# Gating the second pair of start-up loads and reordering the software loads in a fused window-attention and feed-forward kernel

## The chip, the cores and the metric

The kernel runs on one core of one Trainium2 chip. The metric is the device time of one launch in microseconds (us). Before the change it is 303.25 us, the median of four runs (303.24, 303.24, 303.26 and 303.73).

## The reference, cut to what matters

Batch 8, 8 heads, 576 positions, head size 64. Attention sees a window of 32 positions on either side. Its output, 4608 tokens of width 512, goes through a feed-forward pair with a squared ReLU between the two products.

```python
scores = q @ k.T / sqrt(64)                      # per batch and head
scores = where(abs(i - j) <= 32, scores, -1e9)
x = softmax(scores) @ v                          # -> (4608, 512), heads side by side
h = x @ w_in                                     # 512 -> 2048
out = (maximum(h, 0) ** 2) @ w_out               # 2048 -> 512, float32
```

## The kernel before, in words

Attention is cut into 72 chunks of 64 tokens (nine per batch element), the feed-forward part into nine tiles of 512 tokens (T = 0 to 8). An 8th of a tile's x is one chunk.

For a piece of tokens, K and Q (float32 in memory) are loaded with tokens on partitions, turned by TensorE (`tok_turn`, L489) and copied to `kt` by VectorE (L505) and to `qt` by ScalarE (L502) in the first batch element. Scores of a chunk or of two chunks are 8 or 16 small matmuls (L585), ScalarE takes the exponential (L605), VectorE multiplies with the mask (L614), TensorE multiplies with V (L720 and L721), VectorE divides by the row sum (L731, L733) and TensorE and ScalarE turn the result into `xt` (L749, L755). For odd chunks V is needed shifted by 64 partitions: VectorE copies it from `vx` to `vd` (L543, `vd_half`). The first feed-forward tile is made of 16 blocks of 16 matmuls (`mm1_small`, L768): block (g, q) takes 128 tokens (two chunks) and a quarter q of `w_in`; ScalarE's ReLU (L776) and VectorE's square (L824) follow. Then comes the second product (L861), which needs the quarters of `w_out`.

All work is recorded first (`Prog.rec`, L62) with the engine, a planned duration, tags of what it reads and writes, and a key. A planner (`schedule`, L265, with `forward`, L98) simulates five engines and the DMA queues with the durations and the `move` numbers of the loads, tries several priorities, and keeps the order per engine that its own model likes best. After that the order on each engine is fixed: every engine runs its list in order and waits on semaphores. Planned gaps on TensorE up to the first product's dense stretch are filled with idle matmuls on zeros (`fill`, L306, issued as L410); their number follows from the plan, not from what happens on the chip.

Loads use three queues. SyncE (SP) and ScalarE (ACT) issue hardware-queue loads: `first_load` (L449, issued at L454) brings K and Q of piece 0 (96 tokens) and of piece 2 (128 tokens) in float32 into staging tiles (`oe` for piece 0, `pf` for piece 2). GpSimd (POOL) issues all the other loads of batch elements 0 and 1, which convert to bfloat16 on the way: K and Q pieces (L461), V pieces (L531) and the quarters of the two weights (L548, L553). Their order on POOL is the list ORDER (L34): `k03` is K of batch 0, piece 3 in numbers from 0, `w10` the first quarter of `w_in`, `w20` that of `w_out`, and so on. Keys below -100 are kept as they are, so POOL issues them in that order. In batch 0 the pieces are 96, 64, 128, 128, 128 and 32 tokens of K and Q (L38), and 96, 128, 128, 128 and 96 of V (L39). `build` (L895) records all of it.

Before the change both hardware loads of a queue are issued one straight after the other at the start.

Of the kernel before, what the change touches and what calls it, by code (L numbers as in the profile page):

```python
# [30 lines left out]
PADS, MARGINS, ROUNDS, NREP = (0, 1000, 2000), (0, 4000, 8000), 3, 4  # L31
LATE = {"POOL": 1500, "SP": 2000, "ACT": 2000}
DEPTH, POST, BACK = 4000, {"POOL": 1500, "SP": 1000, "ACT": 1000}, {"POOL": 2500, "SP": 4000, "ACT": 4000}
ORDER = ("k01 q01 v00 v01 v02 w10 k03 q03 v03 k04 q04 v04 w11 w12 w13 k05 q05 k10 q10 v10 k11 q11 v11 "  # L34
         "w20 w21 w22 w23 k12 q12 v12 k13 q13 v13 k14 q14 v14").split()
GT0, WT0 = (12.5, 16, 20, 25.5), (13, 18, 23, 26)
TURN0 = {1: 1, 2: 2, 4: 3, 6: 4}
# [321 lines left out]
class Gen:  # L359
# [86 lines left out]
    def slot(self, b, x):  # L446
        return 512 * (x if b else x - 1)

    def first_load(self, t, x, eng, key):  # L449
        t0, n = PIECE0[x]  # L450
        src = (self.q if t == "q" else self.k)[0, :, t0:t0 + n, :].rearrange("h p d -> p h d")
        stg, o, w, tag = self.STG[t, x]
        dst = bass.AP(stg, o, [[w, n], [64, 8], [1, 64]])
        self.p.rec(eng, lambda e: e.dma_start(dst, src), writes=[tag], dma=(f"s{t}{x}", 0), key=key, dur=420, move=(n // 2, 14, 1500 if x == 0 else 2500))  # L454

    def tok_load(self, b, t, x, key):
        t0, n = self.pieces(b)[x]
# [88 lines left out]
    def load_w1(self, d, key):  # L546
        src = self.w_in[:, 512 * d:512 * d + 512].rearrange("(f p) c -> p f c", p=128)
        self.p.rec("POOL", lambda e: e.dma_start(self.W1[:, :, 512 * d:512 * d + 512], src),  # L548
                   writes=[("w1", d)], dma=(f"w1{d}", 0), key=key, dur=770, move=(32, 82 if d else 130, 500))

    def load_w2(self, d, key):
        src = self.w_out[512 * d:512 * d + 512, :].rearrange("(k p) c -> p k c", p=128)
# [342 lines left out]
    def build(self):  # L895
        p = self.p
        self.k1 = self.grp = 0
        self.group, self.bank = {}, {}

        K = -200.0  # L900
        self.setup_idle()
        self.setup_masks(K - 20)
        self.setup_rest(0, K + 3)
        self.setup_ptz(0, K + 2)
        self.setup_ptz(1, K + 2)
        self.setup_ptz(2, K + 2)
        self.setup_rest(1, -20)
        at = {it: K + 1 + k for k, it in enumerate(ORDER)}
        for d in range(4):
            self.load_w1(d, at[f"w1{d}"])  # L910
            self.load_w2(d, at[f"w2{d}"])

        tile = 0
        for b in range(B_):
            while 8 * tile + 7 < NCH * b:
                self.moe(tile)
                tile += 1
            if b < FB:
                if not b:
                    for x in (0, 2):  # L920
                        self.first_load("k", x, "SP", -300 + x)
                        self.first_load("q", x, "ACT", -300 + x)
                for bb in range(0 if b else FB):
                    for x in range(6):
                        for t in "kqv":
                            if f"{t}{bb}{x}" not in at:
                                continue
                            if t == "v":
                                self.vx_load(bb, x, at[f"v{bb}{x}"])
                            else:  # L930
                                self.tok_load(bb, t, x, at[f"{t}{bb}{x}"])
            else:
                for x in range(5):
                    kb = 9 * b - 40 + 2 * x
                    for t in "kq":
                        self.tok_load(b, t, x, kb)
                        self.dma_turn(b, t, x, 9 * b - LEAD - 9 + 2 * x)
                    self.vx_load(b, x, kb + 0.1)
            for c in range(NCH):
                n = NCH * b + c  # L940
                if b >= TB:
                    if c % 3 == 0:
                        if b == 1 and not c:
                            for x in range(2):
                                self.tok_turn(1, x, n - LEAD - 3)
                        self.scores(n, 3)
                        if c == 3:
                            self.vd_half(b, 1, 3, n - LEAD, [("sc", n)])
                        self.av3(n, 0)
                        self.av3(n, 1)  # L950
                        y = (n // 3) % 2
                        self.evac3(n, y)
                        if b == 1 and c < 6:
                            for x in range(2, 4) if not c else (4,):
                                if x < TX:
                                    self.tok_turn(1, x, n - LEAD)
                                else:
                                    for t in "kq":
                                        self.dma_turn(1, t, x, n - LEAD)
                        self.xturn3(n, y)  # L960
                    continue
                m = 1 if not c or n in (1, 8) else 2
                if n not in self.group:
                    if n == 0:
                        self.tok_turn(0, 0, -LEAD - 3)
                    if n == 8:
                        self.moe(0)
                        tile = 1
                        self.tok_turn(0, 5, -LEAD + 5)
                    self.scores(n, m)  # L970
                    if n + m < TB * NCH and n + m != 8:
                        bb, cc = divmod(n + m, NCH)
                        self.tok_turn(bb, (cc + 1) // 2 if bb else TURN0[cc], n + m - LEAD - 3)
                if c % 2 and not b:
                    x = (c + 1) // 2
                    self.vd_half(b, x - 1, x, n - LEAD - 3)
                if b and not self.group[n][1]:
                    odd = [c + u for u in range(self.group[n][2]) if (c + u) % 2]
                    if odd:
                        self.vd_half(b, odd[0] // 2, odd[-1] // 2 + 1, n - LEAD, [("sc", n)])  # L980
                self.av(n)
                gi, k, m = self.group[n]
                if n < 2:
                    self.evac(n, 1, 0, n)
                    if n:
                        self.xturn(0, 2, 0)
                elif k == m - 1:
                    self.evac(n - k, m, gi, 0)
                    self.xturn(n - k, m, gi)

        for T in range(tile, NT + 1):
            self.moe(T)
        p.schedule()
        with self.nc.Block():
            dsems, dcount = p.emit()
            for s in dsems:
                if s[0] == "o":
                    self.nc.sync.wait_ge(dsems[s], dcount[s])
# [32 lines left out]
```

The softmax here doesn't subtract the row's maximum and nothing guards it: scores larger than these inputs give would overflow.

## Time and profile before

| what | value |
|---|---|
| median of the runs shown | 303.25 us |
| the profiled execution's own time | 302.34 us |
| its span, first to last instruction | 300.5 us |
| outside the span | 1.84 us |
| TensorE busy | 293.9 us (98%) |
| VectorE, ScalarE, GpSimd busy | 176.3, 159.9, 105.0 us |
| idle matmuls (L410) | 114, 10.3 us, all between 1.0 and 17.4 us |
| TensorE busy from 25 us to 200 us | 175.0 of 175.0 us |
| software DMA queue | 113120 packets, 17.9 MB |

The profile is one execution with the time of every instruction. "Idle before" is time in which an engine waited ahead of an instruction, with what released it. TensorE counts as busy when it runs idle matmuls too, so in the first 25 us a busy engine is not a useful one. An issue of a load stands on the engine that issues it; a load has landed when its semaphore is complete, which is what the consumer waits for.

Landings in the profiled execution, in us from the start of the span: K and Q of piece 0 at 4.5 and 5.0; of piece 2 at 6.8 and 7.6; k01 7.9, q01 8.1, v00 8.7, v01 9.6, v02 10.4, w10 12.8, k03 13.6, q03 15.4, v03 15.9, k04 16.8, q04 17.6, v04 18.3, w11 20.8, w12 23.3, w13 25.9, w20 33.9, w21 36.6, w22 39.2, w23 42.0, k12 42.7, q12 43.5.

### The profile page before, as it was taken

Reading aid. Unit: us, or ns where it says so; the run is one execution under the profiler, and the core shown is the slowest. Engines: PE = TensorE matmul, PEld = TensorE weight load, DVE = VectorE, ACT = ScalarE, POOL = GpSimd, SP = SyncE. Lnnn points to the kernel's source line nnn. Section 1 sums busy time; section 2 is a strip of 40 time slices with the busy share of each in tenths; the row PEclk is TensorE's granted clock in tenths of the full one; section 3 lists DMA queues with packets and bytes.
Section 4 is the critical chain, followed back from the end, with each engine's and each line's share of the span. In section 5 each row is a group of like instructions: output and inputs, shape, how many; then the busy total and the mean of one; then the engine's idle time right before and its main releaser. Section 6 shows DMA issues by size and latency. Waiting matters only on the chain.

```text
span 300.5 us, 7083 instructions
## 1 busy us (share of the span) xinstructions
PE 293.9 (98%) x2796; PEld 172.1 (57%) x2796; DVE 176.3 (59%) x429; ACT 159.9 (53%) x267; POOL 105.0 (35%) x131
## 2 busy tenths in 40 slices
PE   7889999999999999999999999999999999999996
PEld 7679955866768754444444454444444444444445
DVE  5775656664998957757665596768457663222200
ACT  3457634656758645654565665557365554444411
POOL 8999842241515532452144644315410000000000
PEclk9999999999999999999999999999999999999999
DMA  9999999999999999999899999999992210100022
GB/s 147 174 194 170 206 174 194 170 142 192 175 139 135 122 186 159 129 132 164 141 115 133 156 163 163 130 170 107 158 156 81 79 26 35 37 35 36 35 84 93
DMA packets 166818, 39.34 MB, mean 131 GB/s; under 512 B 157825, under 2 KB 162305, under 8 KB 166785
## 3 DMA queue, kind: packets, MB, share of 16 engines
q0 software_dynamic: 113120, 17.90, 90.3%
q1 hardware_dynamic: 46512, 11.15, 25.6%
q10 hardware_dynamic: 7152, 9.83, 11.2%
q8 instruction: 22, 0.36, 0.5%
q14 instruction: 12, 0.09, 0.1%
HBM read 36.70 MB, written 9.44 MB: 154 GB/s over the span
## 4 chain that ended last, share of the span: by engine, by line
PE 94%; DMA 2%; DVE 2%; issue 0%; ACT 0%; POOL 0%; POOLq 0%; DVEq 0%
PE outp L861 41%; PE ht L809 28%; PE ht L791 7%; PE ht L768 7%; PE sc L585 3%; PE sc L645 3%; DMA kraw<-in_k_dram 2%; PE sc L489 1%; DVE vd L543 1%; PE outp L410 1%; PE sc L837 1%; PE outp L837 1%; DVE kt L505 0%; PE sc L693 0%; PE outp L749 0%
## 5 line engine op out<-in xcount | busy, mean ns | idle before, releaser
L861 PE MATMUL outp<-w,gt 128*128 128x512 bf16 x560 | 136.0, 379 | 0.0
L809 PE MATMUL ht<-xt,w 128*128 128x512 bf16 x384 | 94.5, 379 | 0.0
L824 DVE TENSOR_TENSOR gt<-rt 128x512 bf16<-128x512 bf16 x144 | 59.2, 418 | 58.9 <-ACT rt L815 51.0
L815 ACT ACTIVATE rt<-ht 128x512 bf16<-128x512 f32 x96 | 57.3, 599 | 57.0 <-PE ht L809 54.1
L861 PEld LDWEIGHTS outp<-w,gt 128*128 128x128 bf16 x560 | 52.7, 98 | 58.2
L809 PEld LDWEIGHTS ht<-xt,w 128*128 128x128 bf16 x384 | 36.5, 98 | 42.4
L461 POOL DMA_DIRECT2D qraw<-in_q_dram x39 | 33.2, 852 | 51.7 <-PE ht L809 24.2
L461 POOL DMA_DIRECT2D kraw<-in_k_dram x39 | 33.4, 857 | 44.1 <-PE ht L809 19.3
L605 ACT ACTIVATE e<-sc 128x512 bf16<-128x512 f32 (+1 forms) x48 | 37.4, 809 | 11.5 <-PE sc L585 11.5
L531 POOL DMA_DIRECT2D vx<-in_v_dram x40 | 34.4, 861 | 19.6 <-PE ht L809 10.9
L868 ACT ACTIVATE oe<-outp 128x512 f32<-128x512 f32 x35 | 20.9, 598 | 26.4 <-PE outp L861 26.3
L669 DVE TENSOR_TENSOR xr<-pf,rs 128x512 bf16<-128x512 f32 (+1 forms) x42 | 27.7, 682 | 0.4
L626 DVE TENSOR_TENSOR pt<-e,mask 128x512 bf16<-128x512 bf16 x42 | 17.6, 422 | 14.0 <-ACT e L605 13.9
L768 PE MATMUL ht<-xt,w 128*128 128x128 bf16 x384 | 24.1, 219 | 0.3 <-ACT xt L755 0.3
L791 PE MATMUL ht<-xt,w 128*128 128x256 bf16 x192 | 23.4, 273 | 0.0
L768 PEld LDWEIGHTS ht<-xt,w 128*128 128x128 bf16 x384 | 21.7, 98 | 0.8 <-ACT xt L755 0.5
L662 DVE COPY pf<-sc 128x520 f32<-128x520 f32 x21 | 14.7, 700 | 11.5 <-PE sc L645 11.2
L791 PEld LDWEIGHTS ht<-xt,w 128*128 128x128 bf16 x192 | 18.0, 98 | 3.3
L776 ACT ACTIVATE rt<-ht 128x512 bf16<-128x512 f32 x24 | 14.2, 599 | 10.3 <-PE ht L768 10.0
L659 ACT ACTIVATE pf<-sc 128x520 f32<-128x520 f32 x21 | 12.6, 601 | 11.8 <-PE sc L645 11.8
L797 ACT ACTIVATE rt<-ht 128x512 bf16<-128x512 f32 x24 | 14.4, 599 | 7.4 <-PE ht L791 7.1
L664 DVE TENSOR_TENSOR pf<-pf 64x520 f32<-64x520 f32 x21 | 14.6, 698 | 5.6 <-ACT pf L659 4.7
(78 smaller groups left out, 192.0 us busy)
## 6 DMA issues: line engine op xcount, KB each, us to landing
out_dram<-oe ACTq DMA_DIRECT2D x35, 256.0 KB, 3.6
kraw<-in_k_dram POOLq DMA_DIRECT2D x30, 128.0 KB, 5.7
qraw<-in_q_dram POOLq DMA_DIRECT2D x30, 128.0 KB, 5.4
vx<-in_v_dram POOLq DMA_DIRECT2D x24, 128.0 KB, 5.7
w<-in_moe_w_in_dram POOLq DMA_DIRECT2D x4, 512.0 KB, 10.4
w<-in_moe_w_out_dram POOLq DMA_DIRECT2D x4, 512.0 KB, 16.8
vx<-in_v_dram POOLq DMA_DIRECT2D x16, 96.0 KB, 5.8
xt<-xr SPq DMA_TRANSPOSE x36, 4.4
```

The source lines that it names most:

```text
L461: self.p.rec("POOL", lambda e: e.dma_start(dst, src), writes=[("fraw", b, t, x)], old=[("fraw", b - 2, t, y + (b == 2))], reads=self.pace( ...
L531: self.p.rec("POOL", lambda e: e.dma_start(self.VX[b % 2][r:r + n, s, :, 0:64], self.v[b, :, t0:t0 + n, :].rearrange("h p d -> p h d")), w ...
L605: self.p.rec("ACT", lambda e, d=dst, a=src: e.activation(d, a, ACTF.Exp, scale=0.125), reads=["s" + x for x in name], writes=[("e", h)], k ...
L626: self.p.rec("DVE", lambda e, a=pt, c=ee, d=mb: e.tensor_tensor(a, c, d, ALU.mult), reads=[("e", k // 2), "mask"], writes=[("ptt", k)], ol ...
L669: self.p.rec("DVE", lambda e, w=w, np=np: e.tensor_tensor(bass.AP(self.XR, 512 * (2 * y + w), [[2048, np], [64, 2], [128, 4], [1, 64]]), b ...
L768: mm = e.matmul(ht[:, 128 * (d % 4):128 * (d % 4) + 128], self.W1[:, ft, 128 * d:128 * d + 128], self.XT[:, ft, t0:t0 + 128], start=(ft == ...
L791: mm = e.matmul(ht[:, 256 * (d % 2):256 * (d % 2) + 256], self.W1[:, ft, 128 * d:128 * d + 128], self.XT[:, ft, 64 * s0:64 * s0 + 256], st ...
L809: mm = e.matmul(ht[:], self.W1[:, ft, 128 * d:128 * d + 128], self.XT[:, ft, 512 * T:512 * T + 512], start=(ft == 0), stop=(ft == 3))
L815: self.p.rec("ACT", lambda e: e.activation(rt[:], ht[:], ACTF.Relu), reads=[("ht", k % 2)], writes=[("rt", k % 4)], key=key, dur=560)
L824: self.p.rec("DVE", lambda e: e.tensor_tensor(g, r, r, ALU.mult), reads=[("rt", k % 4)], writes=tags, key=key, dur=430)
L861: mm = e.matmul(op, gt[:, d, 128 * u:128 * u + 128], self.W2[:, d, :], start=(d == 0), stop=(d == 15))
L868: self.p.rec("ACT", lambda e: e.activation(oe[:], op, ACTF.Copy), reads=[tag], writes=[("oe", x % 4)], key=key, dur=560)
```

## The change

The hardware load of piece 2 now waits, on each of the two queues, for the landing of the load of piece 0 on the same queue (the new argument `gate` makes it read the tag of the first staging tile). In ORDER, `k03 q03 v03` move ahead of `w10`, and `w11` moves ahead of `v04`. The planner is told a smaller cost for the first quarter of `w_in` (105 for 130). As the planner runs again with this, the order on all engines comes out new, mostly in the first 40 us.

```diff
-ORDER = ("k01 q01 v00 v01 v02 w10 k03 q03 v03 k04 q04 v04 w11 w12 w13 k05 q05 k10 q10 v10 k11 q11 v11 "
+ORDER = ("k01 q01 v00 v01 v02 k03 q03 v03 w10 k04 q04 w11 v04 w12 w13 k05 q05 k10 q10 v10 k11 q11 v11 "
...
-    def first_load(self, t, x, eng, key):
+    def first_load(self, t, x, eng, key, gate=()):
...
-        self.p.rec(eng, lambda e: e.dma_start(dst, src), writes=[tag], dma=(f"s{t}{x}", 0), key=key, dur=420, move=(n // 2, 14, 1500 if x == 0 else 2500))
+        self.p.rec(eng, lambda e: e.dma_start(dst, src), reads=gate, writes=[tag], dma=(f"s{t}{x}", 0), key=key, dur=420, move=(n // 2, 14, 1500 if x == 0 else 2500))
...
-                   writes=[("w1", d)], dma=(f"w1{d}", 0), key=key, dur=770, move=(32, 82 if d else 130, 500))
+                   writes=[("w1", d)], dma=(f"w1{d}", 0), key=key, dur=770, move=(32, 82 if d else 105, 500))
...
-                    for x in (0, 2):
-                        self.first_load("k", x, "SP", -300 + x)
-                        self.first_load("q", x, "ACT", -300 + x)
+                    self.first_load("k", 0, "SP", -300)
+                    self.first_load("q", 0, "ACT", -300)
...
+                if not b:
+                    self.first_load("k", 2, "SP", -298, [self.STG["k", 0][3]])
+                    self.first_load("q", 2, "ACT", -298, [self.STG["q", 0][3]])
```

In the order that the planner now gives (from the built program): on ScalarE the list begins with the load of piece 0, the gated load of piece 2, the load of the activation table, then the copy to `qt` of piece 0. On VectorE the copies L543 that wait for v00 and v01 stand ahead of the first masking L614. On TensorE the turning of piece 1 stands ahead of the first scores, the first two chunks are done ahead of Q of piece 2, and 86 idle matmuls are left of 114.

## The prediction

> **What bounds the kernel now.** I read the slices first, then TensorE's timeline of the first 25 us, then ScalarE's, then the DMA view by stretches.
>
> ```profile
> PE   7889999999999999999999999999999999999996
> ```
>
> From the fifth slice on TensorE is full, and the table by stretches has it busy 175 of 175 us from 25 to 200. The work after that is fixed, so the change can only move the moment at which the dense stretch begins. That beginning, on TensorE:
>
> ```profile
> 6.60 0.23 PE L410 MATMUL outp<-zz 128*128 128x128 bf16 x1
> 7.93 0.29 PE L489 MATMUL sc<-identw,kraw 64*128 64x64 bf16 x4 [1.09 <-DMA kraw<-in_k_dram]
> ...
> 8.60 1.04 PE L489 MATMUL ht<-oe,pf 128*128 128x128 f32 x8
> ...
> 10.93 0.41 PE L585 MATMUL sc<-qt,kt 64*128 64x64 bf16 x16
> ...
> 15.42 1.06 PE L768 MATMUL ht<-xt,w 128*128 128x128 bf16 x16
> 16.32 1.17 PE L410 MATMUL outp<-zz 128*128 128x128 bf16 x18
> 17.32 0.39 PE L489 MATMUL outp<-identw,kraw 128*128 128x128 bf16 x4
> ...
> 22.21 1.07 PE L768 MATMUL ht<-xt,w 128*128 128x128 bf16 x16
> ```
>
> The columns are start, length, what. TensorE waits for k01 until 7.9; the first feed-forward block stands at 15.42; then come idle matmuls until piece 3, whose q03 landed at 15.4; the second block is at 19.54 and the third, the first to need w11 (landed 20.8), at 22.21. From there TensorE doesn't stop. I measure everything by this third block.
>
> Two views show why k01 is late. By queue (packets, MB, share of the engines), between 4.5 and 5.5 us and between 8 and 9 us:
>
> ```profile
> q10 hardware_dynamic: 423, 0.11, 68.0%
> q1 hardware_dynamic: 412, 0.10, 67.0%
> q0 software_dynamic: 29, 0.00, 5.6%
> ```
>
> ```profile
> q0 software_dynamic: 1226, 0.15, 242.7%
> ```
>
> While the four hardware loads run, the software queue moves 29 packets in a microsecond; alone it moves 1226. A packet is one head of one token: k01 and q01 are 512 each, v00 768, v01, v02, k03 and so on 1024 (0.83 us at that rate). k01's last packet went at 6.7, although GpSimd had issued it by 2.2. ScalarE:
>
> ```profile
> 1.20 0.65 ACTq L454 DMA_DIRECT2D pf<-in_q_dram  x1
> 1.88 1.28 ACT L502 ACT_TABLE_LOAD   x1 [1.88 <-issue]
> 5.74 0.49 ACT L502 ACTIVATE qt<-ht 128x384 bf16<-128x384 f32 x1 [2.59 <-PE ht L489]
> ```
>
> The table load follows the second load's issue in ScalarE's list; today it is over at 3.2 and hidden.
>
> [...] Between 54.5 and 55 us it does (210 packets of q1, 209 of q0); between 4.5 and 5.5 it did not (835 to 29), and the output store issued at 45.55 behind a long software queue sent its first packet only at 49.5. So what entered first seems to go first, and the measurement decides. [...] The trace shows idle matmuls 112 ns apart in the first 4 us and 55 ns apart at 10 us, and no return after the 1.1 us wait.
>
> **The change part by part.**
>
> *Gate on SP.* Nothing else stands on SP's queue until its first transpose at 49 us, so the wait costs no one. K of piece 0 lands at 4.5; today 1.06 us pass from issue (0.74) to the first packet (1.80), so K of piece 2 starts near 5.6 and not 3.6.
>
> *Gate on ACT.* Queued behind it are the table load and everything after. Wait to 5.0, issue 0.65, table load 1.28: 6.95. The copy to `qt` of piece 0 moves from 5.74 to 6.95 and ends at 7.45; first scores 7.6 (today 6.38); exponential of chunk 0 8.0 to 8.55, of chunk 1, after scores at 8.65, 9.0 to 9.6. So the first masking can't be before 8.6.
>
> *Software queue.* The first loads' 1536 packets are through by 4.0. k01 (issued 1.35) then runs 4.0 to 4.45, q01 to 4.9, v00 to 5.5. Landing is 0.7 to 1.2 us after the last packet (v01: 8.64, 9.64), so k01 5.5, q01 5.9, v00 6.5. For v01 the trace has no case of a hardware load arriving at this point. It is issued at 3.6, and after idle stretches a software load starts 1.6 to 2.05 us later, so its first packet is at 5.2 to 5.65, just when K of piece 2 arrives. Bound below: v01 goes whole, last packet 6.4, landed 7.2 to 7.4. Bound above: it shares with both hardware loads to the end, last packet near 8.4, landed 9.4. I take the middle, V = 8.3 (today 9.6). All packets up to v02 are the same work as before, so v02 ends near 9.7 as today. After it: k03, q03, v03 without w10's 2.2 us ahead of them land at 11.4, 12.6, 13.2 (13.6, 15.4, 15.9); w10 behind those three lands at 15.4 (12.8); k04, q04 as today; w11 without v04's 0.6 us ahead at 20.1 (20.8); v04 near 20.6.
>
> *The new chain*, walked along the orders of the built program with durations of this trace. VectorE now has three instructions ahead of the first masking that must be done once v01 is in: two copies L543, 0.95 us together. From V:
> - masking V+1.0 to V+1.4; product with V to V+1.7; row sum, second masking to V+2.5; 12 idle matmuls to V+2.35; turning of K of piece 2, four matmuls, half of the 1.04 us row, to V+2.85; second product V+2.85; Q of piece 2 V+3.1 to V+3.6.
> - kt copy 0.69, row sum, one L543, division 0.42: V+4.7; turning of x L749 0.4; scores of chunks 2 and 3 at V+5.1 (V+5.1 = 13.4; today 10.93, because they stood ahead).
> - 7 idle matmuls; ScalarE's `xt` copy 0.6; piece 3 turned at V+5.9; exponential 1.02, qt copy 0.6; scores of 4 and 5 at V+7.5 = 15.8 (today 18.78).
> - products of 2 and 3, first feed-forward block at V+8.3 = 16.6 (w10 is in at 15.4); divisions 0.2 and 0.69; turning; `xt`; piece 4 at V+10.5 = 18.8 (q04 17.6); second block V+10.95.
> - gt 0.43, row sum, division 0.69, kt copy 0.42, scores of 6 and 7 at V+11.95, turning, third block at V+12.55 = 20.85, w11 just in.
>
> Today's third block is at 22.21, but one turning (4 matmuls, 0.22) comes after it that now comes before, so the equal point is 22.43. Gain 22.43 - 20.85 = 1.6. The path through ScalarE (8.6 for the masking) decides only for V under 7.6. The 28 idle matmuls fewer are no gain of their own; they are gaps not planned.
>
> *What is late next.* Weights and pieces of batch 1. w23 landed at 42.0 and is used at 43.86 (four matmuls into the row at 43.00): a gain over 1.8 would be waited away there. Piece 2 of batch 1 (q12 43.5, used 44.7) is now behind eight matmuls L861 in place of four, 0.86 more. Later scores have 9 us of slack (transposed at 61.9, used at 71.7). If sharing is less efficient than running apart, all landings shift by up to 0.5 and that limit is 1.3. I take a gain of 1.5: 302.34 - 1.5 = 300.84 for a profiled execution (the span 299.0, with 1.84 around it), 0.91 under the median of the runs as today, so 303.25 - 1.5 = 301.75.
>
> *Planner cost 105 for 130*: no instruction; its effect is in the orders walked above.
>
> **Rivals.**
> - *v01 late.* The second loads take the queue as the first did, v01 lands at 9.4 to 9.6. The third block is at 22.0 to 22.15: gain 0.3 to 0.4, 302.9. For it: 835 packets to 29. Against: those hardware loads were issued ahead of the software ones; these are issued behind.
> - *Second loads late, slower.* The gated loads stand behind the software queue as later hardware loads do: transposes issued at 55.5 and 57.0 landed 9.1 and 9.3 us later. At TensorE the turning of K of piece 2 stands ahead of the second product, so a late K stops everything. With 9 us, K lands at 13.6; that takes the place of V+2.35, so V counts as 11.2 and the third block is at 23.8: 1.4 slower, 304.65. It decides from K's landing at 12.2 (no gain) on; over 12.9 it is slower by over 0.2%. Against: at 5 us GpSimd has issued four loads, of which 1.5 us of packets are left, where at 45 us there were 4; this gives landings of 9 to 11.5.
> - *More.* v01 whole ahead and w23 earlier than thought: gain 2.1, 301.15.
> - *The clock falls back* in the thin stretch from 9 to V+1.45. With V = 8.3 the wait is 0.8 us, less than today's 1.1; for the late case it is 1.9. It only worsens that case, by up to 1.5.
> - *The gate does nothing*, because v01 is bound by GpSimd's issue: excluded above 7.4 by its start of 3.6.
>
> **Numbers.** What a measurement of this kernel tells from no change is about 0.2%, 0.6 us. Forecast (gain 0.9 to 1.9) 0.57; v01 late (-0.3 to 0.8) 0.24; second loads late 0.14; more 0.05. Faster by over 0.2%: 0.57, 0.05 and a fifth of the late case, 0.67. Slower: most of the third, 0.13. Same: 0.20. For the range I leave out the best 0.05 and most of the slower case: 301.2 to 303.7.
>
> **What would show it.** Right: k01 landed near 5.5, first packet of K of piece 2 near 5.6, table load at 5.7, qt copy at 6.95, v01 landed between 7.4 and 9, first masking 1 us after that, w10 at 15.4 with the first block at 16.6, third block near 20.9, dense from there with no wait at w23. Wrong: v01 at 9.5; K of piece 2 after 11; TensorE waiting for w10 or w11; a stop near 42 us; idle matmuls at 112 ns again after 10 us.

## The result, and the profile after

| | before | after |
|---|---|---|
| median of the runs measured side by side | 303.25 us (63 runs, 301.94 to 304.86) | 304.38 us (44 runs, 302.71 to 307.05) |
| ratio to before, with its 95% interval | | 1.0038 [1.0027, 1.0049] |
| the profiled execution | 302.34 us | 303.98 us |
| first instruction of the second product L861 | 37.63 us | 39.05 us |
| runs by mean granted clock of TensorE | 1.000 or 0.999 in 61, 0.994 in 14 (the 75 runs taken beside e1 to e4) | 1.000 in 1, 0.994 in 20, 0.989 in 23 |

The kernel became slower by about 1.1 us; forecast was a gain of 1.5. A mean clock of 0.994 is one stretch of 3.41 us at half clock within 302 us (11.06 to 14.48 in the profile of after), 0.989 is two (7.7 to 14.5 in that of e2); below such a stretch is called cold. The one run of after without a cold stretch took 302.87 us, the median with one is 303.79 and with two 304.71. The slices of the profile of after show first that the stretch from the fifth slice on is as full as before, and second a 7 in the row of the granted clock, which stands in the second slice (7.6 to 15.1 us). In before that row has only nines.

```profile
PE   7689999999999999999999999999999999999996
...
PEclk9799999999999999999999999999999999999999
```

TensorE's timeline of after (start, length, what, idle time before it and who ended it):

```profile
8.21 0.29 PE L410 MATMUL outp<-zz 128*128 128x128 bf16 x2
11.14 0.24 PE L720 MATMUL sc<-vx,pt 128*128 128x65 bf16 x1 [2.65 <-DVE pt L614]
...
11.57 1.47 PE L410 MATMUL outp<-zz 128*128 128x128 bf16 x12
12.84 1.06 PE L489 MATMUL ht<-oe,pf 128*128 128x128 f32 x4
...
18.88 1.05 PE L768 MATMUL ht<-xt,w 128*128 128x128 bf16 x16
...
23.21 1.95 PE L768 MATMUL ht<-xt,w 128*128 128x128 bf16 x32
```

Both chunks' scores are done by 8.5, and then TensorE waits 2.65 us for the masking L614. The 12 idle matmuls after the wait take about 0.11 us each (1.27 us from their start to that of the next row), where before had 0.06: the clock has halved. By windows, with the busy time, the number of instructions in brackets and then the granted clock:

```profile
4.24:7.65 3.41, 2.73 (x44) 1.00 1.55 123
7.65:11.06 3.41, 0.85 (x17) 1.00 1.83 191
11.06:14.48 3.42, 3.34 (x35) 0.50 1.88 181
```

In before the masking of the first chunk stood ahead of the copies on VectorE (timeline of before):

```profile
8.46 0.42 DVE L614 TENSOR_TENSOR pt<-e,mask 128x512 bf16<-128x512 bf16 x1
...
9.96 0.98 DVE L543 COPY vd<-vx 64x528 bf16<-64x528 bf16 x2
```

Now it waits behind the copies of v01, as the timeline of after shows:

```profile
6.82 0.42 DVE L543 COPY vd<-vx 64x528 bf16<-64x528 bf16 x1 [1.29 <-DMA vx<-in_v_dram]
7.17 0.27 DVE L505 COPY kt<-sc 128x256 bf16<-128x256 bf16 x1
9.57 1.06 DVE L543 COPY vd<-vx 64x528 bf16<-64x528 bf16 x2 [2.13 <-DMA vx<-in_v_dram]
10.66 0.43 DVE L614 TENSOR_TENSOR pt<-e,mask 128x512 bf16<-128x512 bf16 x1
```

v01 landed at 9.54, where before had 9.64. ScalarE, which the gate was to delay, is no part of this: the exponential of the first chunk was over at 7.9.

```profile
4.64 0.41 ACTq L454 DMA_DIRECT2D pf<-in_q_dram  x1
5.08 1.28 ACT L502 ACT_TABLE_LOAD   x1 [5.08 <-DMA oe<-in_q_dram]
6.37 0.49 ACT L502 ACTIVATE qt<-ht 128x384 bf16<-128x384 f32 x1
```

Why v01 is late is in the DMA view of after between 6.5 and 7.5 us (packets, MB, share of the engines):

```profile
q0 software_dynamic: 426, 0.05, 83.2%
q1 hardware_dynamic: 339, 0.09, 58.8%
q10 hardware_dynamic: 81, 0.02, 9.1%
```

Piece 0 is through at 3.9, and the software queue then has the engines to itself (882 packets between 4.5 and 5.5 us, none of another queue) until the gated loads arrive (first packet of K of piece 2 at 6.17, of Q at 6.72). From there on it shares with them, and its part shrinks to 426 and then 188 packets a microsecond. The same view between 7.5 and 8.5 us:

```profile
q1 hardware_dynamic: 434, 0.11, 62.3%
q10 hardware_dynamic: 368, 0.09, 42.7%
q0 software_dynamic: 188, 0.02, 35.5%
```

So v01's 1024 packets went from 5.84 to 8.67, where in before they went from 7.80 to 8.64 with no hardware load beside them.

### The profile page after: what moved, and what is told of

It is laid out like the page before. It is cut to its first block, busy times and chain, and to the rows that moved or that the text cites. A ratio compares the mean times of both kernels' runs of the same rounds, so it can differ in the third digit from the quotient of the medians.

```text
span 302.2 us, 7034 instructions
## 1 busy us (share of the span) xinstructions
PE 294.4 (97%) x2768; PEld 172.0 (57%) x2768; DVE 176.8 (59%) x429; ACT 160.4 (53%) x267; POOL 105.3 (35%) x131
## 4 chain that ended last, share of the span: by engine, by line
PE 94%; DMA 2%; ACT 1%; DVE 1%; POOL 1%; issue 1%; POOLq 0%
PE outp L861 40%; PE ht L809 28%; PE ht L791 7%; PE ht L768 6%; PE sc L645 3%; PE sc L585 3%; DMA vx<-in_v_dram 2%; PE sc L489 1%; PE outp L410 1%; PE sc L720 1%; ACT e L605 1%; PE sc L837 1%; PE outp L837 1%; PE sc L693 0%; PE ht L489 0%
## 5 line engine op out<-in xcount | busy, mean ns | idle before, releaser
L861 PE MATMUL outp<-w,gt 128*128 128x512 bf16 x560 | 138.0, 379 | 0.0
L809 PE MATMUL ht<-xt,w 128*128 128x512 bf16 x384 | 96.5, 379 | 0.0
L861 PEld LDWEIGHTS outp<-w,gt 128*128 128x128 bf16 x560 | 52.5, 98 | 57.7
L461 POOL DMA_DIRECT2D qraw<-in_q_dram x39 | 33.9, 870 | 49.8 <-PE ht L791 16.3
L461 POOL DMA_DIRECT2D kraw<-in_k_dram x39 | 34.1, 874 | 41.5 <-PE ht L809 21.2
L531 POOL DMA_DIRECT2D vx<-in_v_dram x40 | 35.2, 881 | 26.5 <-PE ht L809 9.5
```

Source lines behind the costliest of these rows:

```text
L461: self.p.rec("POOL", lambda e: e.dma_start(dst, src), writes=[("fraw", b, t, x)], old=[("fraw", b - 2, t, y + (b == 2))], reads=self.pace( ...
L531: self.p.rec("POOL", lambda e: e.dma_start(self.VX[b % 2][r:r + n, s, :, 0:64], self.v[b, :, t0:t0 + n, :].rearrange("h p d -> p h d")), w ...
L809: mm = e.matmul(ht[:], self.W1[:, ft, 128 * d:128 * d + 128], self.XT[:, ft, 512 * T:512 * T + 512], start=(ft == 0), stop=(ft == 3))
L861: mm = e.matmul(op, gt[:, d, 128 * u:128 * u + 128], self.W2[:, d, :], start=(d == 0), stop=(d == 15))
```

## The experiments

Theory after the result: the gate brings k01, q01 and v00 as forecast, but v01 shares the engines with the gated loads; VectorE's new order puts v01's copies ahead of the first masking; the wait halves TensorE's clock, and that is the larger part of the loss. Rivals: the gate itself costs (K and Q of piece 2 are late), the new order itself costs, or the wait alone costs and the clock only shows it.

Each is measured against before on the same chip. In e1 to e7 and e12 the edit leaves the planner's orders as they are (apart from what it moves itself); where "planned again" stands, the orders are new on all engines. Some of the edits are shown in part, with three dots for what is left out. Line numbers move by a few with the edits.

**e1, the gate alone, in the orders of before**

```diff
         p.schedule()
+        by = {o.dma[0]: o for o in p.ops if o.dma is not None and o.dma[0] in ("sk0", "sq0", "sk2", "sq2")}
+        by["sk2"].deps.add(by["sk0"])
+        by["sq2"].deps.add(by["sq0"])
```

> The kernel before with its orders on all engines unchanged; only the second hardware load on each queue waits for the first to land. Theory (the gated loads land late, near 10.3 and 10.8 us, and whoever stands in line behind them waits): k01 lands near 5.1, but the turning of piece 2, which in this order stands ahead of the first products with V, waits until 10.8 in place of 8.6, the clock falls back once, the third feed-forward block comes at about 24.2: some 2 us slower, 305. Rival (the gate is good and the new orders are the loss): the early k01 carries through, third block before 22.2, time under 303.25.

Measured: 304.73 us, ratio 1.0067 [1.0047, 1.0086]; 21 of 22 runs have one or two cold stretches. K and Q of piece 2 landed at 9.81 and 12.56, TensorE waited for both, and v01 landed at 9.64. TensorE's timeline of e1:

```profile
9.85 0.66 PE L489 MATMUL ht<-oe,pf 128*128 128x128 f32 x4 [1.32 <-DMA pf<-in_k_dram]
12.61 1.12 PE L489 MATMUL ht<-oe,pf 128*128 128x128 f32 x4 [2.10 <-DMA pf<-in_q_dram]
```

In the orders of before the gate costs some 1.5 us, the clock included.

**e2, the new orders without the gate**

```diff
         p.schedule()
+        for o in p.ops:
+            if o.dma is not None and o.dma[0] in ("sk2", "sq2"):
+                o.deps = set()
```

> The kernel after with its orders unchanged, its second hardware loads issued at the start again as before. Theory (the first masking waits in line behind the copies of v01, and v01 lands at 9.5 with or without the gate): k01 lands at 7.9 again, v01 at 9.6, first masking at 10.7, a wait of over 2 us on TensorE ahead of it, third block within 0.4 us of the changed kernel's 23.2; time 304 to 304.5, not different from the changed kernel. Rival (the gate is what costs, by delaying v02, w10 and w11 by about 0.6 to 1 us and piece 2 to 10.8): 303 or less.

Measured: 304.80 us, ratio 1.0058 [1.0040, 1.0076]. The time was near the expected one, but it came from another wait: q01 landed at 7.99 and TensorE waited 2.43 us for it, since the new order turns piece 1 ahead of the first scores. The clock was halved from 7.7 to 14.5, and the third block came at 23.95, 0.74 later than in after. TensorE's timeline of e2:

```profile
8.04 0.39 PE L489 MATMUL sc<-identw,qraw 64*128 64x64 bf16 x4 [2.43 <-DMA qraw<-in_q_dram]
```

Each half alone costs as much as both together: with the gate alone piece 2 comes late for the old orders, with the orders alone q01 comes late for the new ones. So the loss is not a sum of two parts, and neither half alone is its cause.

**e3, the changed kernel with the wait filled**: 44 more idle matmuls ahead of the first product with V.

```diff
+HOLD = 44
...
-            for k in range(int((gap - 60) * (DENSE if at < COLD else SPARSE) // one) + (EXTRA if op is self.first and op.start < self.idle_end.start else 0)):
+            for k in range(int((gap - 60) * (DENSE if at < COLD else SPARSE) // one) + (EXTRA if op is self.first and op.start < self.idle_end.start else 0) + (HOLD if op is self.hold else 0)):
...
+        if not n:
+            self.p.hold = op
```

> The kernel after with 44 more idle matmuls on zeros ahead of the first product with V, in the wait from 8.5 to 11.1 us, nothing else changed. Theory (the clock halves because TensorE idles there, and each cold window of 3.4 us costs about 0.9): mean granted clock 1.000, av and turnings after 11 us at full pace, third block 1.0 to 1.3 us earlier near 22.0, time 302.7 to 303.1. Rival (the chain is bound by v01 alone and the cold stretch costs nothing that isn't waited for anyway): clock 1.000 but time within 0.3 of 304.4.

Measured: 302.50 us (22 runs, 301.76 to 303.01), ratio 0.9980 [0.9966, 0.9994]; mean clock 1.000 in all 22. The landings that the first masking and piece 2 wait for are within 0.5 us of after's (v01 9.40, K and Q of piece 2 9.84 and 11.23), and the masking starts at 10.64, as in after. In TensorE's timeline of e3 the idle matmuls take 0.06 us each, which is the full pace:

```profile
8.51 2.74 PE L411 MATMUL outp<-zz 128*128 128x128 bf16 x46
...
22.39 1.95 PE L771 MATMUL ht<-xt,w 128*128 128x128 bf16 x32
```

The third feed-forward block comes 0.82 us earlier than in after and the second product L861 1.21 us earlier, with nothing taken off the chain. The profiled execution is 302.47 us, 1.51 less than after's and 0.13 more than before's. So the clock, and not the wait itself, is what makes after slower; without it the two kernels are the same within the measurement by their profiles.

**e4, v01's two copies behind the first division on VectorE**: after the planner, the two L543 that wait for v01 are moved behind the first L733 (tag 1 marks the two copies, tag 2 that division).

```diff
         p.schedule()
+        late = [o for o in p.ops if getattr(o, "tagged", 0) == 1]
+        last = next(i for i, o in enumerate(p.ops) if getattr(o, "tagged", 0) == 2)
+        rest = [o for o in p.ops if getattr(o, "tagged", 0) != 1]
+        at = rest.index(p.ops[last]) + 1
+        p.ops = rest[:at] + late + rest[at:]
```

> The kernel after with two VectorE copies that wait for v01 moved from ahead of the first masking to behind the first division; all other orders unchanged, gate kept. Theory (VectorE's line behind v01 is the loss): first masking near 8.0, first product with V near 8.5 and no wait over 2 us there, clock 1.000, second product near 11 (bound by v01 at 9.5 and K of piece 2 at 10.3), third block at w11's landing near 21.4; time 302.2. Rival (piece 2's late landing, 10.3 and 10.8, is the bound): third block not before 22.5, time 303.3 or more.

Measured: 303.92 us, ratio 1.0021 [1.0002, 1.0040], mean clock 1.000 in 12 of 22 runs. The masking came at 8.31, 2.3 us earlier than in after. In TensorE's timeline of e4 this took its place:

```profile
11.88 0.66 PE L489 MATMUL ht<-oe,pf 128*128 128x128 f32 x4 [0.68 <-DMA pf<-in_q_dram]
```

Q of piece 2, which the gate had delayed (it landed at 11.83 here), is next; the third block is at 22.32, hardly earlier than in e3 (22.39). The profiled execution then loses another 1.1 us at 88.7, waiting for a transposing DMA (`xt<-xr`), and 0.5 at 214.8 for a transposed Q, which e3 doesn't. What made those transfers late was not tried.

**e5, half of the wait filled**: e3 with 20 in place of 44.

```diff
-HOLD = 44
+HOLD = 20
```

> The changed kernel with 20 more idle matmuls, not 44, ahead of the first product with V. 44 of them took 2.5 us, so 20 fill some 1.2 us of the 2.65 us wait and leave 1.45 us. Theory (the clock falls for the sparse stretch as a whole, and the kernel before with waits of 1.1 us kept its clock in most runs): most runs keep the full clock and end near the run with the whole gap filled, 302.5 to 303.0 us; a minority has one cold stretch. Rival (any wait over about 1 us at this place makes the clock fall): cold in nearly all runs, 303.8 to 304.4 us.

Measured: 302.91 us, ratio 1.0023 [1.0009, 1.0037]; 16 of 22 runs have clock 1.000 and a median of 302.64, six have 0.994 and a median of 304.42. In the profiled execution TensorE waited 2.02 us in one piece (from 9.86 to 11.88) and the clock stayed, as the windows of e5 show:

```profile
4.78:8.20 3.42, 2.74 (x42) 1.00 1.43 131
8.20:11.61 3.41, 1.63 (x30) 1.00 1.92 178
11.61:15.02 3.41, 2.99 (x50) 1.00 1.81 186
```

The two heaps of this one kernel (a heap is a group of runs with nearly the same time) price a cold stretch at 1.8 us. It doesn't cost that each time: one of the six cold runs took 302.65.

**e6, before with its own wait filled** (18 more idle matmuls ahead of the turning of K of piece 1, `fill` changed as in e3), as a fair partner of e3.

```diff
+HOLD = 18
...
+            if not b and x == 1 and todo[0][0] == "k":
+                self.p.hold = self.p.ops[-1]
```

> The kernel before with 18 more idle matmuls ahead of the turning of K of piece 1, so that its 1.1 us wait for k01 is filled too; nothing else changes. It is the fair partner of the run of the changed kernel with its gap filled (302.50 us). Theory (the changed kernel without its cold stretch is about 0.75 us better by its loads and order): the clock is full in nearly all runs and the time stays at 303.0 to 303.25 us. Rival (the filled run won only because no run of it is cold, and the order of loads is worth nothing): 302.4 to 302.6 us.

Measured: 303.19 us, ratio 1.0008 [0.9991, 1.0025]; all 14 runs at clock 1.000. But the runs lie in two heaps, five at 302.24 to 302.63 and nine from 303.0 on, and so do before's (302.3 and 303.25, both at full clock). So the median suits the theory, and the profiles (e6 302.24, e3 302.47) suit the rival: what e3 is better by depends on the heap it is held against. The upper heap became a question of its own (e10, e13).

**e7, the gate moved to v01**: both loads of piece 2 on SyncE's queue, waiting for v01.

```diff
         p.schedule()
+        v01 = next(o for o in p.ops if o.dma == ("vf01", 0))
+        for o in p.ops:
+            if o.dma is not None and o.dma[0] in ("sk2", "sq2"):
+                o.deps, o.eng = {v01}, "SP"
```

> The changed kernel with both loads of piece 2 on SyncE's queue, waiting for v01 in place of the first loads; so nothing of the hardware queues moves while v01 does, and ScalarE is not held. Theory (v01 lands at 9.5 because it shares the engines with the gated loads): v01 lands at 7.3 to 7.9, the first masking is near 8.5 to 9. Rival (v01's landing is set by its own queue and issue, whatever the hardware queues do): it lands at 9.2 to 9.6 as in every run so far. In both cases K and Q of piece 2 come 6 us after v01, at 13.5 or later, and the run is slower than after, 305 us or more.

Measured: 309.76 us (two runs). VectorE's timeline of e7:

```profile
7.56 0.95 DVE L543 COPY vd<-vx 64x528 bf16<-64x528 bf16 x2
8.55 0.42 DVE L614 TENSOR_TENSOR pt<-e,mask 128x512 bf16<-128x512 bf16 x1
```

v01 landed at 7.40, 2.1 us earlier than in after, and the masking came at 8.55. That settles why v01 is late in after. The price was expected: K of piece 2 landed at 13.3, Q, second on the same queue, at 17.85, and TensorE waited 3.2 and 3.0 us for them.

**e8, the list of loads alone** (planned again, no gate).

```diff
-ORDER = ("k01 q01 v00 v01 v02 w10 k03 q03 v03 k04 q04 v04 w11 w12 w13 k05 q05 k10 q10 v10 k11 q11 v11 "
+ORDER = ("k01 q01 v00 v01 v02 k03 q03 v03 w10 k04 q04 w11 v04 w12 w13 k05 q05 k10 q10 v10 k11 q11 v11 "
...
-                   writes=[("w1", d)], dma=(f"w1{d}", 0), key=key, dur=770, move=(32, 82 if d else 130, 500))
+                   writes=[("w1", d)], dma=(f"w1{d}", 0), key=key, dur=770, move=(32, 82 if d else 105, 500))
```

> The kernel before with the new list of loads and the planner's new cost for the first quarter of the weights, planned again, without the gate. Theory (the start of the dense stretch hangs on v01, piece 2 and w11, which the list alone does not bring earlier): 302.8 to 303.6 us, not different from before, at full clock in most runs because K and Q of piece 2 are turned in the thin stretch. Rival (the list carries the gain and the gate spoils it): 302.3 us or less. A third outcome, w10 at 16 or later ahead of the first block with nothing to do before it: 304 us or more.

Measured: 302.32 us, ratio 1.0003 [0.9988, 1.0019]; 13 runs at clock 1.000 (median 302.31) and nine at 0.994 (303.88). No difference from before.

**e9, the same with its wait for q01 filled**: e8 with the edit of e6, 20 idle matmuls ahead of the turning of Q of piece 1.

```diff
+HOLD = 20
...
+            if not b and x == 1 and todo[0][0] == "q":
+                self.p.hold = self.p.ops[-1]
```

> The new list of loads alone, planned again, without the gate, and with 20 more idle matmuls at the wait for q01 ahead of the turning of piece 1 (1.26 us in the run of the list alone). There 13 of 22 runs had the full clock and took 302.31 us, 9 had one cold stretch and took about 303.9. Theory (the cold stretch is the whole difference between these two heaps): all runs at full clock, 302.3 us, and lower than before's mean of 302.7 to 303.1. Rival (the runs at 303.9 are late in something else and cold for that reason, a late landing of q01): two heaps stay.

Measured: 302.40 us, ratio 1.0003 [0.9983, 1.0023]; eight runs at 1.000 (median 302.28), six at 0.994 (303.92). The rival holds: filling that one wait doesn't empty the upper heap. Which idle stretch it comes from was not found.

**e10 and e11, before once more, for its profile**, e10 without an edit, e11 with a constant that nothing reads.

> The kernel before once more, for its profile alone. Its runs lie in two heaps, 302.3 and 303.25 us, both at full clock. If this run is of the upper heap, its trace shows where the 0.95 us are: either in the first 25 us (a landing that is late, so that the third feed-forward block is at 23.2 in place of 22.2) or at a later stop. If it is of the lower heap, nothing is learned.

> The kernel before a third time, as the run ahead of this one, for a second chance of a profile of the upper heap. Same expectation.

Measured: e10 303.23 us, so of the upper heap; e11 302.35. The third block is 0.95 us later in e10 (23.16 for 22.21), as was thought possible, but no late landing made it so: those that the chain uses (k01 to w10, w11) are within 0.3 us of before's. The lateness comes out of one kind of instruction on VectorE. The view of the tile `vd` between 8 and 14 us, for before (number of copies, then shortest, median and longest in ns):

```profile
L543 DVE COPY vd<-vx x5: 292/294/661, 10.0 to 13.0; 64x528 bf16<-64x528 bf16 x5
```

The same view for e10:

```profile
L543 DVE COPY vd<-vx x5: 506/660/837, 9.8 to 13.7; 64x528 bf16<-64x528 bf16 x5
```

The same copy takes 0.29 us or up to 0.84. The five sum to 2.17 us in before and 3.30 in e10; they begin 0.17 earlier there, which leaves 0.96. e11, of the lower heap, has before's durations but for the first copy (0.46).

**e12, before with 31 idle matmuls fewer** between 10.05 and 13.6 us, so that no wait there is long (`gaps` counts the stretches that `fill` fills).

```diff
+THIN = (7, 8, 9)
...
+            gaps += n > 0
+            for k in range(0 if n > 0 and gaps in THIN else n):
```

> The kernel before without the 31 idle matmuls that stand between 10.05 and 13.6 us (14, 2 and 15 of them): TensorE then has waits of about 0.9, 1.1 and 1.3 us there, with 0.4 us of real work between them, and no landing or other engine is touched. Theory (what lets the clock fall is one unbroken wait of over 2 us): full clock in most runs, as before. Rival (what counts is the busy share of the stretch of some 3.4 us, here about a quarter): the clock halves in most runs and the time grows by 1 to 1.9 us, as in the changed kernel.

Measured: 304.64 us, ratio 1.0063 [1.0039, 1.0088]; no run of seven at 1.000. The longest wait is 1.59 us, shorter than the 2.02 of e5. The windows of e12:

```profile
7.31:10.73 3.42, 2.28 (x34) 1.00 2.02 174
10.73:14.14 3.41, 0.82 (x24) 1.00 1.95 173
14.14:17.55 3.41, 2.73 (x34) 0.50 2.26 168
```

My theory of one long wait falls, and the rival fits: in the stretch ahead of the half clock TensorE was busy for 0.82 us of 3.41, where e5 had 1.63 and kept its clock. (This profiled execution is 2.3 us behind before's: it also has the long copies, 0.48, 0.74, 0.50, 0.66 and 0.55 us.)

**e13, before with five copies L543 on ScalarE**, planned again.

```diff
+LAST = 2
...
-            self.p.rec("DVE", lambda e, d=dst, c=src: e.tensor_copy(d, c), reads=rd,
...
+            a = not b and s0 + lo <= LAST
+            self.p.rec("ACT" if a else "DVE", lambda e, d=dst, c=src, a=a: e.activation(d, c, ACTF.Copy) if a else e.tensor_copy(d, c), reads=rd,
```

> The kernel before with the first five copies of V into vd on ScalarE in place of VectorE, planned again. Theory (in kernel before the two heaps at full clock, 302.3 and 303.25 us, come from these copies on VectorE, which last 0.29 us or up to 0.84 us while GpSimd issues loads, and they stand in the chain from the first division to the second product): one heap at full clock, at 302.0 us or lower, since 1.3 to 2.1 us of copies leave VectorE's chain and some 1.2 us of copies on ScalarE stand ahead of the second product. Rival (the copies are only where the lateness shows, and another wait takes their place at the second product): the two heaps stay, or one heap at 302.3 us or above.

Measured: 301.64 us (seven runs, 301.62 to 301.88), ratio 0.9959 [0.9938, 0.9981], all at clock 1.000 and in one heap. It beats both kernels. As the planner ran again, the other orders may differ too, so not all of the gain need be the copies' own. ScalarE's copies take some 0.64 us each and there is room for them, as its timeline of e13 shows:

```profile
10.82 1.31 ACT L545 ACTIVATE vd<-vx 64x528 bf16<-64x528 bf16 x2
```

On TensorE the second product of e13 starts at 11.52 (before 12.33), and only just waits for them:

```profile
11.52 0.20 PE L722 MATMUL sc<-vd,pt 128*128 128x65 bf16 x1 [0.15 <-ACT vd L545]
```

**e14, the changed kernel with the three copies of v00 and v01 on ScalarE**, planned again (the edit of e13 with `LAST = 1`).

> The changed kernel with the three copies that read v00 and v01 on ScalarE, planned again, so that the first masking on VectorE waits for neither. Theory (with v01 at 9.5 us what costs is only the wait of TensorE behind these copies and the clock that it loses): the first product is at 8.8 us in place of 11.1, most runs keep the clock, third feed-forward block at 22.0 to 22.4, 302.3 to 302.8 us. Rival (K and Q of piece 2 at 10.3 to 11.8 and the second exponential, which now stands behind the copies on ScalarE, set the second product): no better than the run with the copies behind the masking on VectorE, 303.3 to 304 us.

Measured: 303.68 us, ratio 1.0028 [1.0014, 1.0043], 19 of 22 runs at 1.000. The first product no longer waits, but the second exponential stands behind the copies and the second masking comes at 11.64; the third block is at 22.32, as in e4 and near e3's. The rival holds. The profiled execution loses 2.4 us more after 87 us, 1.4 of them in the same wait for `xt<-xr` as in e4.

## Why the prediction was wrong, point by point

- *What bounds the kernel*: right. The start of the dense stretch set the time; the 1.42 us at the first L861 grow to 1.64 at the end.
- *Gate on SP and ACT*: right, and cheaper than thought. k01 landed at 5.05 (forecast 5.5), the table load ended at 6.36 and the copy to `qt` began at 6.37 (6.95), because Q of piece 0 landed at 4.61 and not 5.0 and the issue took 0.41 us and not 0.65. K of piece 2 had its first packet at 6.17 (5.6).
- *Software queue*: mis-sized. k01, q01 and v00 were to be through at 5.5, at 1226 packets a microsecond. Their 1792 packets went from 3.43 to 5.87, so v01's first packet was at 5.84 and not between 5.2 and 5.65. The 29 packets were read where two hardware loads were under way (4.5 to 5.5 us, piece 0 being through by 4.1), not four as I wrote. How queues share was open: in before they moved alike between 54.5 and 55 us (210 packets of q1, 209 of q0), and 835 to 29 between 4.5 and 5.5. With two hardware loads beside it again, the software queue moved 426 and then 188 in after: its share is not one number.
- *"I take the middle, V = 8.3"*: this is the step that failed. v01 landed at 9.54, 0.14 above my upper bound. The lower bound was right (7.40 without the hardware loads in e7), the choice between the two was not: v01 shared to the end, as in the bound above. That took most of the gain: in e3, with v01 at 9.40 and the clock full, the third block is at 22.39 (forecast 20.85, equal point 22.43), 1.10 us of it from v01 and 0.44 from the chain behind it. I had seen that all packets up to v02 are the same work as before, and did not draw the line at v01: v01's packets fell from 426 to 188 a microsecond as those of K and Q of piece 2 rose from 420 to 802, and the second product needs all three. Nor did that work end when it had: in before the last packet of the three was v01's, at 8.64, and v02's went at 9.65; in after v01's was at 8.67, v02's at 10.31 and Q's at 10.39.
- *The rival "the clock falls back"*: right in mechanism, about right in size, and left without a chance of its own. I wrote that for the late case the wait is 1.9 us and costs up to 1.5; the 1.5 was my estimate, and no trace of before showed it. It was 2.65 us, as the scores of both chunks were done by 8.5, and e3 prices it at 1.51 us by the profiles and 1.9 by the medians. "v01 late" gave 302.9; with 1.5 for the clock that is 304.4, and 304.38 was measured. I had named both and not put them together: 43 of the 44 runs of after have a cold stretch. That the sum meets the median so closely is in part luck, as the median lies between runs with one cold stretch (303.79) and with two (304.71).
- *The chain from V*: right at full clock. In e3, with V = 9.40, the masking is at V+1.24 (forecast V+1.0; the two copies took 1.19 us and not 0.95) and the third block at V+12.99 (V+12.55). In after it is at V+13.67; the rest is the clock.
- *Weights*: mis-sized. I let v02 end as before and the landings shift by up to 0.5; v02 landed 0.9 later, w10 at 17.27 (forecast 15.4), w11 at 21.39 (20.1) and w23 at 42.89 (before 42.0). None of it was waited for ahead of the third block.
- *"Second loads late"*: K and Q of piece 2 landed at 10.30 and 10.76, inside the 9 to 11.5 forecast, and were not late as long as v01 was. With v01 at 8.3 my chain would have needed K at 10.65 and Q at 11.4, so with after's landings they were in time. But Q's landing moves from run to run (10.76 in after, 11.83 in e4), and in e4, where the masking didn't wait for v01, TensorE waited 0.68 us for Q and the third block was at 22.32, nearly where it had been. So the gain of 1.5 was likely not to be had by an early v01 alone; that was not run.
- *The offset of 0.91 between the profile and the median*: it is the distance of before's two heaps, of which the profile shows the lower. Held against the lower heap, after is 2.06 us slower.

What stays open: why the transposing DMA at 88 us is late in e4 and e14 and not in after and e3, and where the cold runs of e8 and e9 come from. No run with v01 early and piece 2 in time was tried.

## What to carry to other kernels

When a change moves transfers among queues that slow each other (here 426 packets a microsecond fell to 188 beside two hardware loads), list every load that the next step needs and ask which is last, with all packets counted that are under way beside it. The gate brought k01 2.8 us earlier and v01 only 0.1, because the gated loads then ran beside v01 (with none beside it, in e7, v01 landed at 7.40 and not 9.54). Rival mechanisms that feed each other (a late load, and a clock that falls in the wait it makes, here 2.65 us of wait and 1.51 us for the clock) need a case of their own with both costs added. And look at the spread of one small instruction before moving big ones: the kernel with five copies taken off VectorE gained 1.6 us against before's upper heap and 0.7 against its lower, where the new list of loads alone (e8) gained nothing.

## What the runs showed of the hardware that was not expected

**The clock fell after stretches of 3.41 us with little work in them (0.23 to 1.58 us, once 2.12).** In after the half clock lasts from 11.06 to 14.48, 3.42 us, and in e2 from 7.7 to 14.5, about twice that. With stretches of 3.41 us laid off from the clock's own changes, TensorE's busy time in the one ahead of a fall was 0.85 us in after, 0.82 in e12, 1.34 in e2, 1.58 in e1 and 0.23 in e7. Ahead of no fall it was 1.63 in e5, 1.85 in e4, 1.94 in e10 and 2.27 at the least in before. One case doesn't fit: in e8 a stretch with 2.12 us was followed by the half clock. Nor does the busy share tell when the full clock comes back: after had it again after a stretch with 3.34 us busy, e12 after one with 2.73, and e2 not after one with 3.06. The slow pace of the start ends at 4.93 in before and at 6.03 in e10, the same kernel: two idle matmuls took 0.28 us at 5.09 in before, and 0.42 at 5.23 in e10. So the place of the stretches that are laid off from there differs between runs of one kernel. Whether that is why one kernel has runs with no, one or two cold stretches (after: 1, 20 and 23 runs) was not shown.

**The same copy on VectorE took 0.29 us or up to 0.84 while GpSimd was issuing loads.** GpSimd's issues in the timeline of before (its copies stand in the section on the result):

```profile
10.42 0.91 POOL L531 DMA_DIRECT2D vx<-in_v_dram  x1
11.31 2.26 POOL L548 DMA_DIRECT2D w<-in_moe_w_in_dram  x3
```

The same of e10, with its first two copies:

```profile
9.79 1.61 DVE L543 COPY vd<-vx 64x528 bf16<-64x528 bf16 x2
10.41 0.87 POOL L531 DMA_DIRECT2D vx<-in_v_dram  x1
11.18 2.33 POOL L548 DMA_DIRECT2D w<-in_moe_w_in_dram  x3
```

In eleven profiles a copy L543 that began anywhere from 9.77 to 10.18 ended at 10.61 to 10.63, 0.2 us after GpSimd began an issue at some 10.42. The next one, at 10.66, took 0.29 us in before, e6 and e11, and GpSimd's following issue began at 11.30; in e10 and e12 it took 0.74, and that issue began at 11.18. That GpSimd issues loads is not enough to make a copy long: in before the one of 0.29 us, from 10.66 to 10.95, lies inside the issue of 10.42 to 11.33. Which of the two engines waits for the other, and whether before's two heaps, 0.95 us apart, come from that, was not shown: no run moved GpSimd's work. e13 took the copies off VectorE and had one heap (301.62 to 301.88 us).
